# Reordering the first two units of a fused attention and two-layer kernel

## The chip, the core and the metric

One Trainium2 (trn2) chip, one core. The metric is the device time of one execution in microseconds (us); 521.43 us is the median of three runs of the kernel before (520.35 to 522.20). Engines: PE (TensorE), DVE (VectorE), ACT (ScalarE), POOL (GpSimd), SP (SyncE, which here only issues DMAs). Each takes its instructions strictly in the order in which they stand in its queue.

## What is computed

A recurrent gated attention over 2 batches, 8 heads, 768 steps and 40 channels, and then two feed-forward layers over the resulting 1536 rows of 320 channels, with 1536 hidden channels each:

```python
for t in range(S):                       # attention, per batch and head
    m_new  = max(f[t] + m, i[t])
    f_stab = exp(f[t] + m - m_new); i_stab = exp(i[t] - m_new)
    C = f_stab * C + i_stab * outer(v[t], k[t]);  n = f_stab * n + i_stab * k[t]
    y[t] = sigmoid(o[t]) * (C @ q[t]) / max(abs(n @ q[t]), 1)
x  = y as rows;  xn = x / rms(x) * rms_g
x2 = (silu(xn @ w_gate) * (xn @ w_val)) @ w_out          # first layer
out = (sigmoid(x2 @ w2_gate) * (x2 @ w2_val)) @ w2_out   # second layer
```

## The kernel before

**Units.** The attention is cut into 12 units: 6 chunks of 128 steps, times 2 batches; unit u is chunk u // 2 of batch u % 2. A unit loads its operands (`a_load`: qk, nat, qt), turns gate sums into weights (`a_bcast_pe`, then `a_exp`; chunk 0 uses `a_bcast0`/`a_bcast0b`), multiplies queries by keys on PE (`a_scores`, L323), weighs the scores on DVE (`a_weigh`, L330), multiplies by the values (`a_out`, L343), makes its addition to the running state (`a_wv` on POOL L289, `a_state` on PE L368, `a_update` on DVE L379), normalises (`a_norm1`, `a_norm1b`, `a_norm1c`, `a_norm2`, `a_norm3`: L391 to L419), is turned by three PE transposes (`a_flip`, L423 to L425) and split into a high and a low part (`a_xt`: ACT L430, DVE L431 and L432). Two units make one tile `xT` of 256 columns; without both, the first layer can't start on it.

**Gate sums.** Those of chunk 0 are made for u = 0 and 1 at once, those of the other chunks by `g_rest`, cut into three bf16 parts by `g_part` (ACT and DVE), and written by `g_send` (L204) as six small DMAs into `rows3[0]` and `rows3[1]`: in the kernel before the three of batch 0 on SP, the three of batch 1 on POOL. `a_bcast_pe` and `a_scale` read these rows. `g_dec` and `g_cols` make the decay factors and columns for the later chunks.

**Weight words.** Each layer has 12 blocks m of weights, each in two pieces p. A piece is loaded by SP (`w_load`, L95, 544 KB) into one of four buffers `wraw`, unpacked by two ACT passes (`w_pre`: L99 and L106) and a DVE pass (`w_bits`, L110), after which its `wraw` buffer is free, and split into wH on ACT (`w_hi`, L119) and wL on DVE (`w_lo`, L123), after which its `wT` buffer (three of them) is free. So load k + 4 waits for `w_bits` of piece k. Pieces are named (layer, m, p); piece k of the first layer is (0, k // 2, k % 2).

**First layer.** Steps are pairs (group g of 256 rows, block m): 16 `up` matmuls (L460), tanh and products on ACT, DVE and POOL (`act1`), two steps later 6 `down` matmuls (L471 to L473). Groups 0 to 3 each go through all 12 blocks in turn, so in group 0 each step also has to wait for its block's weights.

**What sets the order.** Up to the first matmul of group 0 all engines follow an order written out by hand (L637 to L751). `keep_warm(n)` (L685) puts n matmuls without use into PE's queue; `T["wm"]` has their numbers. After the last instruction of that order on each engine (`marks`) a planner orders everything else at compile time, by due times (`want`) and by its own estimate of when operands are ready; `unit(u)`, `w_step(k)` and the `up`, `down` steps give those due times. PSUM tiles named `at`, `up`, `sc` and `dn` have two buffers each; a new tile takes the one that comes free first.

**Names in the steps.** Units 0 and 1 are chunk 0 of the two batches. In PSUM, `at` holds in turn the outputs of `a_out`, `a_state`, `a_flip` and `g_cols`, and `up` holds both the sums of `a_bcast_pe(2)` and those of the first steps.

Of the kernel before, what the change touches and what calls it, by code (L numbers as in the profile page):

```python
# [16 lines left out]
B, H, S, D = 2, 8, 768, 40  # L17
# [33 lines left out]
    start=9.89, d0=4.6, d1=2.84, d2=5.36, w0=1.9, w1=-11.36, wld=9.1, lead=(33, 35, 35, 35, 42, 60), skew=3.0, stg=1.5,  # L51
    uld=9.62, sl=9.1, fl=-6.46, wm=(6, 5, 4, 8, 4), st=1.2,
    fs=(2, 3, 5, 6, 14, 16),
# [4 lines left out]
def attention_then_two_moe(tc, fi, fir, qk, qt3, nat, w1, w2, rms_g, consts, out):  # L58
# [141 lines left out]
    def g_send():  # L200
        n = H * NR
        for k in range(3):
            for b, q in ((0, nc.sync), (1, nc.gpsimd)):
                q.dma_start(out=rows3[b][k * n:(k + 1) * n].rearrange("p q l -> p (q l)"), in_=parts[b * n:(b + 1) * n, k])  # L204

# [396 lines left out]
    def w_step(k):  # L602
        moe, m, p = piece(k)
        if k < 3:
            return
        t = t_slot(first(moe, None, m)) + T["w1" if moe else "w0"] + p
        if k > 3:
            want(t - T["wld"], lambda: w_load(moe, m, p))
        want(t - 3, lambda: w_pre(moe, m, p))
        want(t - 2, lambda: w_bits(moe, m, p))  # L610
        want(t - 1, lambda: w_hi(moe, m, p))
        want(t, lambda: w_lo(moe, m, p))

    def unit(u):
        t = t_unit(u) + (u % B) * T["skew"]
        st = [
            [a_scale, a_bcast_pe, a_exp],
            [a_scores, a_wv, a_gate],
# [18 lines left out]
    with tc.manual_schedule(engines=set(engines)):  # L637
# [78 lines left out]
        a_weigh(1)  # L716
        a_state(0)
        w_pre(0, 0, 1)
        g_part(1)
        a_norm1b(0)  # L720
        a_norm1c(0)
        g_send()
        a_out(1)
        a_norm2(0)
        w_hi(0, 0, 0)
        a_gate(1)
        w_bits(0, 0, 1)
        a_norm3(0)
        keep_warm(wm[2])
        a_flip(0)  # L730
        a_norm1(1)
        a_norm1b(1)
        a_norm1c(1)
        a_xt(0)
        w_lo(0, 0, 0)
        w_hi(0, 0, 1)
        g_dec()
        a_update(0)
        a_norm2(1)
        w_pre(0, 1, 0)  # L740
        keep_warm(wm[3])
        g_cols()
        a_norm3(1)
        keep_warm(wm[4])
        a_flip(1)
        w_lo(0, 0, 1)
        a_xt(1)
        w_bits(0, 1, 0)
        w_hi(0, 1, 0)
        w_lo(0, 1, 0)  # L750
        marks = [next(i for i in reversed(nc.cur_bb.bb.instructions) if i.engine == e) for e in engines]  # L751

# [113 lines left out]
```

## Time and profile before

| | value |
| --- | --- |
| median of three runs | 521.43 us |
| the profiled execution | 520.35 us |
| its span, first to last instruction | 518.6 us |
| PE busy | 505.1 us, 97% |
| ACT, DVE, POOL busy | 231.3, 261.0, 108.7 us |
| bytes read from HBM | 39.10 MB |
| first `up` matmul | 36.34 us after the start of the span |

The span is what the trace covers; 1.75 us of the profiled execution lie around it. Times in the rows are us from the start of the span. Busy shares are averages over stages that have different limits, so the page's share by engine says little about the first 100 us; the views that cut the span into stretches do. A matmul's shown duration contains a modelled end that overlaps the next one.

### The profile page before, as it was taken

What the parts mean: (1) busy time and instruction counts of PE and PEld (TensorE: products, weight loads), DVE (VectorE), ACT (ScalarE), POOL (GpSimd) and SP (SyncE); (2) the same over time, 40 slices, a digit from 0 to 9 for tenths busy, and PEclk for the clock granted to TensorE, in tenths of its full rate; (3) what the DMA queues carried; (4) which work ended last, traced back from release to release, by engine and by line L of the source; (5) the groups of instructions that cost most, each with busy time, mean ns of one, the idle gap of its engine ahead of it and who ended that gap; (6) DMA issues with size and microseconds to landing.
All of it is one profiled execution on the core that took longest, in us unless ns stands there. A gap on an engine that the chain in (4) does not pass through costs nothing.

```text
span 518.6 us, 9096 instructions
## 1 busy us (share of the span) xinstructions
PE 505.1 (97%) x3592; PEld 467.3 (90%) x3592; DVE 261.0 (50%) x540; ACT 231.3 (45%) x518; POOL 108.7 (21%) x173
## 2 busy tenths in 40 slices
PE   9879998999999999999999999999999999999997
PEld 6758897999999999999999999998888888888997
DVE  5677999643355445547675646523233233222332
ACT  4568998632243233326577556442222222221332
POOL 5432252632233343222221212110000000000000
PEclk9789999999999989999999999999999999999999
DMA  7777878510021020102053341000000010000100
GB/s 235 224 237 239 280 256 274 189 59 1 27 81 55 25 81 15 42 1 87 25 196 126 108 151 44 1 1 25 1 1 2 0 52 0 1 1 0 52 1 25
DMA packets 15366, 41.83 MB, mean 81 GB/s; under 512 B 1898, under 2 KB 6613, under 8 KB 15324
## 3 DMA queue, kind: packets, MB, share of 16 engines
q1 hardware_dynamic: 15036, 40.92, 24.3%
q8 instruction: 28, 0.46, 0.4%
q10 hardware_dynamic: 192, 0.25, 0.1%
q0 software_dynamic: 96, 0.09, 0.1%
q14 instruction: 14, 0.11, 0.1%
HBM read 39.10 MB, written 1.97 MB: 79 GB/s over the span
## 4 chain that ended last, share of the span: by engine, by line
PE 75%; DMA 10%; ACT 8%; DVE 4%; issue 2%; POOL 0%; SPq 0%; ACTq 0%; POOLq 0%
PE up L460 32%; PE sc L460 9%; DMA wraw<-in_w_dram 9%; PE dn L471 5%; PE dn L472 5%; PE dn L473 5%; PE at L343 4%; PE sc L323 3%; ACT wT L99 2%; ACT wH L119 2%; ACT wraw L106 2%; PE dn L685 2%; DVE wT L110 2%; PE at L472 2%; PE at L471 2%
## 5 line engine op out<-in xcount | busy, mean ns | idle before, releaser
L460 PE MATMUL up<-xT,wH 128*128 128x256 f32 x940 | 163.7, 288 | 3.8 <-DVE th L491 1.8
L460 PEld LDWEIGHTS up<-xT,wH 128*128 128x128 f32 x940 | 134.8, 190 | 6.8 <-DVE th L491 3.7
L460 PE MATMUL up<-xT,wL 128*128 128x256 f32 x564 | 101.6, 287 | 0.1
L493 POOL TENSOR_TENSOR hT<-th,hT 128x256 fp32r<-128x256 f32 x72 | 58.5, 813 | 144.7 <-ACT hT L492 105.1
L460 PEld LDWEIGHTS up<-xT,wL 128*128 128x128 f32 x564 | 82.1, 191 | 0.6 <-DVE wL L123 0.3
L471 PE MATMUL dn<-wH,hT 128*128 128x320 f32 x184 | 58.0, 316 | 0.0
L472 PE MATMUL dn<-wL,hT 128*128 128x320 f32 x184 | 57.1, 311 | 0.0
L473 PE MATMUL dn<-wH,hT 128*128 128x320 f32 x184 | 56.3, 314 | 0.7 <-POOL hT L493 0.7
L490 DVE SCALAR_TENSOR_TENSOR th<-th,up 128x256 f32<-128x256 f32 x72 | 30.0, 417 | 53.1 <-ACT th L489 52.6
L544 ACT ACTIVATE th<-up 128x256 f32<-128x256 f32 (+1 forms) x48 | 23.6, 491 | 72.4 <-PE up L460 72.4
L545 DVE SCALAR_TENSOR_TENSOR th<-th,sc 128x512 f32<-128x512 f32 x24 | 16.5, 688 | 64.0 <-PE sc L460 63.9
L546 ACT CAST hT<-th 128x256 fp32r<-128x256 f32 (+1 forms) x48 | 24.6, 513 | 50.8 <-DVE th L545 50.8
L489 ACT ACTIVATE th<-up 128x256 f32<-128x256 f32 x72 | 27.4, 381 | 41.8 <-PE up L460 41.8
L106 ACT ACTIVATE wraw<-wraw 128x544 int32<-128x544 uint16 x48 | 33.9, 709 | 22.6 <-DMA wraw<-in_w_dram 22.5
L492 ACT CAST hT<-th 128x256 fp32r<-128x256 f32 x72 | 29.1, 404 | 32.5 <-DVE th L491 32.5
L547 DVE TENSOR_TENSOR hT<-th,hT 128x256 fp32r<-128x256 f32 (+1 forms) x48 | 28.3, 589 | 25.0 <-ACT hT L546 24.9
L110 DVE SCALAR_TENSOR_TENSOR wT<-wT,wraw 128x544 int32<-128x544 int32 x48 | 36.3, 766 | 5.8 <-ACT wT L99 5.1
L123 DVE TENSOR_TENSOR wL<-wT,wH 128x544 fp32r<-128x544 f32 x46 | 33.2, 755 | 9.8 <-ACT wH L119 9.6
L471 PEld LDWEIGHTS dn<-wH,hT 128*128 128x128 f32 x184 | 34.7, 188 | 1.5 <-ACT hT L492 0.2
L472 PEld LDWEIGHTS dn<-wL,hT 128*128 128x128 f32 x184 | 34.6, 188 | 0.9
L473 PEld LDWEIGHTS dn<-wH,hT 128*128 128x128 f32 x184 | 34.0, 188 | 1.2 <-POOL hT L493 0.9
L99 ACT ACTIVATE wT<-wraw 128x544 f32<-128x544 f32 x48 | 32.9, 703 | 0.4 <-DVE wL L123 0.2
(191 smaller groups left out, 831.1 us busy)
## 6 DMA issues: line engine op xcount, KB each, us to landing
wraw<-in_w_dram SPq DMA_DIRECT2D x48, 544.0 KB
nat<-in_nat_dram SPq DMA_DIRECT2D x12, 324.0 KB
qk<-in_qk_dram SPq DMA_DIRECT2D x24, 160.0 KB
nat<-in_nat_dram SPq DMA_DIRECT2D x12, 180.0 KB
qt<-in_qt_dram SPq DMA_DIRECT2D x10, 180.0 KB
out_dram<-x2n SPq DMA_DIRECT2D x11, 160.0 KB
gB<-in_rms_g_dram SPq DMA_DIRECT2D x1, 160.0 KB
out_dram<-x2n ACTq DMA_DIRECT2D x1, 160.0 KB
```

The costliest lines, as they stand in the source:

```text
L99: nc.scalar.activation(t.bitcast(F32), wraw[moe, m, p][:, :, 1].bitcast(F32), AF.Prelu, scale=2.0 ** -112, alpha=2.0 ** 32)
L106: nc.scalar.activation(raw[:, :, 0], top, AF.Copy, scale=2.0 ** -13, bias=2.0 ** -14 - 0.5)
L110: nc.vector.scalar_tensor_tensor(out=t, in0=t, scalar=3, in1=raw[:, :, 0], op0=ALU.logical_shift_left, op1=ALU.bitwise_or)
L123: nc.vector.tensor_tensor(out=wL[moe, m][:, sl], in0=wT.pop((moe, m, p)).bitcast(F32), in1=wH[moe, m][:, sl].bitcast(F32), op=ALU.subtract)
L460: mm = nc.tensor.matmul(o, lhsT=a, rhs=b, start=(n == 0), stop=(n == 7))
L471: nc.tensor.matmul(o, lhsT=hi, rhs=wo[0], start=first, stop=False)
L472: nc.tensor.matmul(o, lhsT=hi, rhs=wo[1], start=False, stop=False)
L473: pe_last[0] = nc.tensor.matmul(o, lhsT=lo, rhs=wo[0], start=False, stop=last)
L490: nc.vector.scalar_tensor_tensor(out=th, in0=th, scalar=1.0, in1=gt, op0=ALU.add, op1=ALU.mult)
L492: nc.scalar.copy(hT[:, 0, :], th)
L493: nc.gpsimd.tensor_tensor(out=hT[:, 1, :], in0=th, in1=hT[:, 0, :].bitcast(F32), op=ALU.subtract)
L547: nc.vector.tensor_tensor(out=hT[:, 1, :], in0=th, in1=hT[:, 0, :].bitcast(F32), op=ALU.subtract)
```

## The change

In the order written by hand: `a_state(0)` moves from before unit 1's output to after `a_norm1(1)`; `a_norm1b(0)` and `a_norm1c(0)` move behind the output of unit 1 and `w_hi(0, 0, 0)`; the first pass over piece (0, 1, 0) moves forward; the normalisation of unit 1 moves ahead of `a_norm3(0)` and of `w_hi(0, 0, 1)`; `a_bcast_pe(2)` and `a_exp(2)` are taken out of `unit(2)` into the hand order; `g_dec`, `a_update(0)` and `g_cols` move behind `a_xt(1)`; piece (0, 1, 1) is unpacked and split by hand too. All six DMAs of `g_send` are issued by POOL. Of the warm-up matmuls, group 2 has 3 instead of 4 and group 3 has 6 instead of 8.

```diff
-    uld=9.62, sl=9.1, fl=-6.46, wm=(6, 5, 4, 8, 4), st=1.2,
+    uld=9.62, sl=9.1, fl=-6.46, wm=(6, 5, 3, 6, 4), st=1.2,
@@ g_send
-            for b, q in ((0, nc.sync), (1, nc.gpsimd)):
-                q.dma_start(out=rows3[b][k * n:(k + 1) * n].rearrange("p q l -> p (q l)"), in_=parts[b * n:(b + 1) * n, k])
+            for b in range(B):
+                nc.gpsimd.dma_start(out=rows3[b][k * n:(k + 1) * n].rearrange("p q l -> p (q l)"), in_=parts[b * n:(b + 1) * n, k])
@@ w_step
-        if k < 3:
+        if k < 4:
             return
         t = t_slot(first(moe, None, m)) + T["w1" if moe else "w0"] + p
-        if k > 3:
-            want(t - T["wld"], lambda: w_load(moe, m, p))
+        want(t - T["wld"], lambda: w_load(moe, m, p))
@@ unit
-            [a_scale, a_bcast_pe, a_exp],
+            [a_scale, a_bcast_pe, a_exp] if u > B else [a_scale],
@@ the order by hand
         g_part(0)
         a_norm1(0)
         a_weigh(1)
-        a_state(0)
         w_pre(0, 0, 1)
         g_part(1)
+        g_send()
+        keep_warm(wm[2])
+        a_out(1)
+        w_hi(0, 0, 0)
+        a_gate(1)
         a_norm1b(0)
         a_norm1c(0)
-        g_send()
-        a_out(1)
+        w_pre(0, 1, 0)
+        w_bits(0, 0, 1)
         a_norm2(0)
-        w_hi(0, 0, 0)
-        a_gate(1)
-        w_bits(0, 0, 1)
-        a_norm3(0)
-        keep_warm(wm[2])
-        a_flip(0)
         a_norm1(1)
+        a_state(0)
+        keep_warm(wm[3])
         a_norm1b(1)
         a_norm1c(1)
+        a_norm3(0)
+        w_hi(0, 0, 1)
+        a_flip(0)
+        a_norm2(1)
+        w_lo(0, 0, 0)
+        w_pre(0, 1, 1)
         a_xt(0)
-        w_lo(0, 0, 0)
-        w_hi(0, 0, 1)
-        g_dec()
-        a_update(0)
-        a_norm2(1)
-        w_pre(0, 1, 0)
-        keep_warm(wm[3])
-        g_cols()
+        a_bcast_pe(2)
+        keep_warm(wm[4])
         a_norm3(1)
-        keep_warm(wm[4])
         a_flip(1)
         w_lo(0, 0, 1)
         a_xt(1)
+        a_exp(2)
+        g_dec()
+        a_update(0)
+        g_cols()
         w_bits(0, 1, 0)
         w_hi(0, 1, 0)
+        w_bits(0, 1, 1)
         w_lo(0, 1, 0)
+        w_hi(0, 1, 1)
+        w_lo(0, 1, 1)
```

## Rows read from the trace of the kernel before

**Rows 1.** The page, part 1: busy time of PE, share, instructions.

```profile
PE 505.1 (97%) x3592; PEld 467.3 (90%) x3592; DVE 261.0 (50%) x540; ACT 231.3 (45%) x518; POOL 108.7 (21%) x173
```

**Rows 2.** Stretches: window, length, busy us (count) by engine, granted clock, DMA share, GB/s.

```profile
14.00:36.30 22.30, 17.99 (x123) 13.38 (x121) 16.23 (x37) 12.69 (x33) 7.00 (x11) 0.85 0.70 221
...
20.00:26.60 6.60, 6.60 (x26) 4.29 (x26) 3.82 (x11) 3.63 (x10) 0.98 (x1) 0.50 0.89 274
...
36.30:95.80 59.50, 56.85 (x441) 52.17 (x442) 52.27 (x97) 52.32 (x109) 23.07 (x30) 0.97 0.80 261
95.80:250.00 154.20, 154.17 (x1261) 149.14 (x1260) 76.67 (x187) 57.75 (x150) 50.10 (x79) 0.99 0.15 48
```

**Rows 3.** Chain of waits, 14 to 37 us: start, length, engine, tile, line.

```profile
18.15 1.39 issue
...
30.09 0.61 PE at L368 x6
...
31.58 1.09 PE sc L323 x16
32.67 0.32 PE at L297 x3
...
34.64 0.48 PE at L339 x2
35.12 0.21 PE at L368 x2
35.34 0.43 PE at L339 x4
```

**Rows 4.** Timeline to the first up matmul: start, length, engine, line, operation, [idle before].

```profile
13.84 1.88 PE L343 MATMUL at<-nat,E 128*128 128x41 f32 x16
...
16.84 1.29 DVE L330 TENSOR_TENSOR E<-E,sc 128x512 f32<-128x512 f32 x2 [0.16 <-PE sc L323]
...
18.94 0.49 DVE L403 TENSOR_TENSOR y<-at,rd 128x320 f32<-128x320 f32 x1
...
28.46 1.02 DVE L417 SCALAR_TENSOR_TENSOR y<-y,r,gB 128x320 f32<-128x320 f32 x1
...
29.53 0.33 PE L423 MATMUL at<-ident,y 128*128 128x128 f32 x1 [0.71 <-DVE y L417]
...
30.13 0.48 ACT L430 CAST xT<-at 128x384 fp32r<-128x384 f32 x1 [2.81 <-PE at L425]
...
30.64 0.42 DVE L431 TENSOR_TENSOR xT<-at,xT 128x256 fp32r<-128x256 f32 x1 [0.30 <-ACT xT L430]
...
36.34 0.74 PE L460 MATMUL up<-xT,wH 128*128 128x256 f32 x4 [0.59 <-ACT E L307]
```

**Rows 5.** The same timeline, queues of SP (SPq) and POOL.

```profile
16.11 3.22 SPq L204 DMA_DIRECT2D rows<-x2n  x3
...
18.05 0.52 POOL L204 DMA_DIRECT2D rows<-x2n  x1 [0.90 <-ACT x2n L194]
...
18.88 0.51 POOL L204 DMA_DIRECT2D rows<-x2n  x1 [0.31 <-DVE rd L396]
...
28.40 0.73 POOL L289 TENSOR_TENSOR wv<-nat,early 128x328 f32<-128x328 f32 x1
...
30.84 0.35 SPq L249 DMA_DIRECT2D nat<-in_nat_dram  x1
...
32.22 0.33 SPq L95 DMA_DIRECT2D wraw<-in_w_dram  x1
...
35.24 0.35 SPq L95 DMA_DIRECT2D wraw<-in_w_dram  x1
```

**Rows 6.** The same timeline, second weight block on DVE, load 7 on ACT.

```profile
39.28 1.36 DVE L123 TENSOR_TENSOR wL<-wT,wH 128x544 fp32r<-128x544 f32 x2
...
41.37 0.70 ACT L106 ACTIVATE wraw<-wraw 128x544 int32<-128x544 uint16 x1 [1.57 <-DMA wraw<-in_w_dram]
```

**Rows 7.** DMA issues before 110 us: queue, count, KB each, us to landing.

```profile
rows<-x2n POOLq DMA_DIRECT2D x3, 30.0 KB, 1.8
```

## The prediction

> **What bounds the kernel now.** I read the page first: PE is busy 97% of the span [rows 1], which alone would leave almost nothing to gain. So I cut the span into stretches. From 95.8 to 250 us PE is busy 154.17 of 154.20 us [rows 2]: there PE's own work is the bound, and whatever PE has finished earlier comes off the end. From 36.3 to 95.8 us PE is busy 56.85 of 59.5 us at a granted clock of 0.97, while ACT and DVE show 52.3 us each and the DMA engines 80% [rows 2]: weights are unpacked for the first time there, four resources are nearly full together, and none of them has much to give. From 14 to 36.3 us PE is busy 17.99 of 22.3 us (and part of that is warm-up), ACT only 12.69, DVE 16.23 [rows 2]. This is the stretch that the change rewrites. The chain of waits and the timeline then say what PE did in it, and the queue of SP what was waiting behind what.
>
> The Trainium skill, page "Trainium Kernel Development and Optimization", note on reading a trace, says that matmul busy time is a poor measure because matmuls are pipelined; by it 56.85 of 59.5 us may hide further gaps. The trace agrees in so far as a shown duration contains a modelled tail. The sum below does not use it.
>
> **Part 1: `a_state(0)` behind unit 1's output.** Unit 0's output and its state both sit in the two `at` buffers, so unit 1's `a_out` finds none. Its weighing is done at 16.84 + 1.29 = 18.13 us, but the chain shows 1.39 us of "issue" from 18.15, and the buffer's last reader, L403, ends at 18.94 + 0.49 = 19.43 [rows 3, 4]. With the state behind, the output can start at 18.15 and takes the 1.88 us that unit 0's took at full clock [rows 4]: done at 20.0. After that gap the clock of PE is 0.50 from 20 to 26.6 us [rows 2]; whether it stays up now is open, since PE will again be empty for some 2 us before the first turn. The three warm-up matmuls taken away stand where PE waits for DVE and ACT, so I cost them at nothing; what they cover is the clock, and if it is lost, part 2 pays (last paragraph).
>
> **Part 2: normalisation, turn and `xT`, replayed with the old durations.** ACT now runs the first unpacking of (0, 1, 0), two passes of about 0.70 us [rows 6], before `a_norm1(1)`, so unit 1's absolute values come at 21.9 us, not right behind its output at 20.0, and its normalised rows at about 23.5 on DVE. `a_norm3(0)` stands behind these: first turn at about 24.3 us. ACT then takes `w_hi` (about as long as one unpacking pass), waits for the fourth `wT` buffer until `w_lo(0, 0, 0)` is done (25.2), unpacks piece 3 until 26.5, copies unit 0's `xT` until 27.0, and DVE subtracts until 27.7. `a_norm3(1)` follows; in the row its product took 1.02 us while POOL ran L289 beside it [rows 4, 5], and without this neighbour I take 0.55 (bounds 0.55 and 1.02) and 0.2 for the copy: second turn at 28.5 us against 29.53 [rows 4]. So this part gains about 1 us (bounds 0.3 and 1.5).
>
> **Part 3: `a_bcast_pe(2)` and `a_exp(2)` in front, the largest term.** Before, PE did not go from the second turn to `up`. It ran the state of unit 1, scores, scale, and the parts of unit 2, waited for DVE in between, and then needed an `up` buffer that ACT's exponentials still held: `up` starts at 36.34 us and waits for "ACT E L307" at the end [rows 3, 4], though the split of xT was at 30.64 + 0.42 us, with one more subtraction of some 0.3 behind it. Now the broadcast is ahead of the second turn and the exponentials come right after `a_xt(1)` on ACT. From the turn at 28.5: 0.6 for the transposes, 0.48 on ACT, 0.42 and some 0.3 on DVE [rows 4], and by estimate 0.2 for `g_dec` and 0.4 for `g_cols` and hand-overs gives a first `up` at about 31.0 us: 5.3 us earlier. `g_cols` in front of `up` costs some 0.6 of this, as its matmul waits for `g_dec`, which stands behind the split on DVE.
>
> This isn't 5.3 us off the end. What PE did between the turn and 36.34 is still owed: 0.61 (state of unit 1), 1.09 (scores), 0.32 (scale), 0.48 + 0.21 + 0.43 (output and state of unit 2) [rows 3], 3.1 us. Net, PE is ahead by **2.2 us** when it reaches the same point.
>
> **Part 4: the fourth piece.** wL of (0, 1, 1) was finished at 39.28 + 1.36 = 40.6 us at the latest [rows 6]; now DVE and ACT do it right after `g_cols`: bits at 32.3 to 33.0, high part to 33.7, low part to 34.5 us. Block 1 is then 6 us earlier, which the earlier `up` needs. ACT was idle 22.3 - 12.69 = 9.6 us from 14 to 36.3 us [rows 2]; my replay of the new order leaves 7.0 us (1.3 + 1.5 + 0.5 + 2.3 + 1.4 between the steps above), so ACT enters the crowded stretch **2.6 us** ahead. DVE gains 1 to 2 us in the same way. Loads: load 6 waits for the bits of (0, 1, 0), which come at 32.3 as before (its row is 32.22); load 7 goes from 35.24 to 33.0 us, and ACT waited for that one until 41.37 [rows 5, 6]. So weights, ACT and PE are all ahead by about 2 to 2.6 us, DVE a little less.
>
> **Part 5: `g_send` all on POOL.** Before, SP stood in these issues from 16.11 for 3.22 us [rows 5], and load 4 behind it; now load 4 can go at 15.0. Nobody waits for load 4 (its unpacking starts after 33 us), so I cost the gain at nothing. POOL takes three more issues at 0.51 us [rows 5], until 20.1 us, before its power for unit 0 is asked for at 20.9. The last row lands 1.8 us [rows 7] later, at 22; the broadcast that reads it stands behind the turn at 24.3, so 2 us of cover remain.
>
> The Trainium skill, page "DMA: Bandwidth & Descriptors", section on the anatomy of a gpsimd DMA, gives a fit of 2.0 us plus bytes over 436e3 for one such DMA, 2.1 us here (an estimate from that page); were six taken one after the other from 16.4, the last would land at 28.8 and hold the broadcast by over 3 us. The rows speak against that: the second and third of POOL's issues start 0.83 us apart, 0.52 and 0.51 us long [rows 5], and the three land in 1.8 us at the median [rows 7], so they overlap.
>
> **The sum.** PE ahead by 2.2, ACT by 2.6, DVE by 1 to 2, and from 95.8 us on the lead is kept. I take 2.4 us, as PE and ACT are the two fullest: the profiled execution would go from 520.35 to 517.95. It lies 1.08 us under the median of the runs shown, so for the median 521.43 - 2.4 = **519.0 us**. A measurement of this kernel can tell about 0.3%, 1.56 us, from no change.
>
> **Rivals.**
> *The reserve goes too.* PE shows 59.5 - 56.85 = 2.65 us idle and loses 3% of 59.5 us, 1.8 us, to the clock in the crowded stretch [rows 2]. If blocks 1 to 3 being early removes this, 4.4 us come on top of 2.4 at most: 514.6, I take 515.5. Against it: ACT and DVE are themselves almost full there. Chance 0.10.
> *The lead is given back.* The planner makes a new order for everything behind the hand order, with the same due times, and DVE or the DMA engines, at 80% [rows 2], let later blocks come when they did: PE only waits in another place. Then 521.4. For it: all four are within 12% of each other. Chance 0.24.
> *Weights queue behind `nat` on SP (slower).* Unit 3's `nat` load waits for the state of unit 1, and in the row it stands ahead of load 6 on SP: 30.84, then 32.22 [rows 5]. POOL's L289 for unit 1 now has to follow the two selects of `a_exp(2)`, about 31.7 us, so the state comes at about 33.2, `nat` takes SP until 34.1, and load 6, if it stays behind, goes out 1.9 us late. Weights then set the pace, the early `up` gains nothing, and the end moves to 523.3. It decides if the planner keeps that order and `nat` is free later than 32.3 us. Against it: load 6 has the earlier due time, and will now be ready first. Chance 0.18.
> *The change does not start `up` earlier*, because the planner or a buffer keeps other work ahead of it, belongs to the second rival; its share there is small.
>
> **Chances and range.** The forecast (517.2 to 520.2) has 0.48, the reserve 0.10, given back 0.24, slower 0.18. Faster by over 0.3% (under 519.87): most of the first and all of the second, 0.56. Within 0.3%: 0.26. Slower: 0.18. The range goes from 515.2, which takes in most of the second case, to 522.9, all of "given back" and the edge of the slower one; about a fifth stays outside.
>
> **What would show it.** Right: first `up` near 31 us, no "issue" gap before unit 1's output, second turn near 28.5, wL of (0, 1, 1) before 35, load 6 ahead of unit 3's `nat`, and the end of group 0 (95.8 before) at 93 to 94 us. Wrong: `up` at 31 but the dense stretch still beginning near 96 (given back), or load 6 after 33.5 us (the queue on SP), or a broadcast that waits for the rows. The replay takes the old durations and the clock as it was; if PE stays at 0.50 longer than from 20 to 26.6 us, turns and broadcast come later, and part 2 loses up to 1 us.

## The result, and the profile after

The changed kernel takes **526.34 us** (median of 4 runs, 523.77 to 529.24) against 520.89 us of before beside it (518.49 to 522.20): ratio 1.010, 95% interval 1.005 to 1.015. It is slower by 1%; forecast were 519.0 us, and 515.2 to 522.9 as the range. Ratios, here and below, are the record's estimates over the fast runs and not quotients of the two medians, which take in every run. Its profiled execution took 527.93 us, span 526.2 us, so 7.6 us more span than before.

What the change was to do at the start, it did. Four lines of the timeline after (start, length, engine, line, operation, idle time before it and what ended it):

```profile
18.43 3.47 PE L343 MATMUL at<-nat,E 128*128 128x41 f32 x16
...
25.64 0.38 PE L277 MATMUL up<-pick,rows 120*128 120x512 bf16 x1 [0.21 <-DMA rows<-x2n]
...
28.32 0.30 PE L423 MATMUL at<-ident,y 128*128 128x128 f32 x1 [0.78 <-DVE y L417]
...
29.91 0.74 PE L460 MATMUL up<-xT,wH 128*128 128x256 f32 x4 [1.07 <-ACT E L307]
```

Unit 1's output starts without the 1.39 us of "issue" of [rows 3], the second turn stands at 28.32 us (29.53 in [rows 4]), and the first `up` at 29.91 us, 6.4 us ahead of [rows 4]. Step 1 of group 0 still starts 3.3 us ahead, at 37.16 us (before: 40.45), but step 2 only at 48.28 (before: 45.13). The same view:

```profile
37.16 1.20 PE L460 MATMUL up<-xT,wH 128*128 128x256 f32 x4
...
48.28 1.20 PE L460 MATMUL up<-xT,wH 128*128 128x256 f32 x4
```

Where the time is lost is best read from when each group's result is written into `x2n`, from the timelines of ACT (us from the span's start; the changed kernel is called "after"):

```
                       group 0  group 1  group 2  group 3  group 4    end of span
before                   101.7    148.5    204.1    246.6    340.5       518.6
after                    110.0    154.0    209.4    252.4    347.9       526.2
```

8.3 us are lost in group 0, 2.8 come back in group 1, 1.6 go in group 4. Part of the 8.3 us is only a shift: when group 0 is written, PE has done 702 matmuls after and 659 before, warm-ups left out, and 38 of the 43 more are the attention's. (The 95.8 us that the prediction calls the end of group 0 is the first `up` of group 1, at 95.86 before; after, it stands at 103.03.) Now the stretches of [rows 2] in the kernel after, with 30 to 60 us in slices of 10 us (window, length, busy us of PE, PEld, DVE, ACT, POOL, granted clock, DMA share, GB/s):

```profile
14.00:36.30 22.30, 20.24 (x123) 16.59 (x123) 15.03 (x37) 13.29 (x34) 9.00 (x15) 0.73 0.59 175
30.00:40.00 10.00, 10.00 (x57) 9.35 (x58) 7.88 (x17) 6.42 (x13) 3.36 (x5) 0.56 0.43 136
40.00:50.00 10.00, 10.00 (x69) 8.59 (x67) 6.41 (x12) 7.58 (x15) 3.94 (x5) 0.84 0.78 248
50.00:60.00 10.00, 10.00 (x60) 8.91 (x60) 7.48 (x13) 6.05 (x13) 1.83 (x3) 0.75 0.61 205
36.30:95.80 59.50, 58.03 (x416) 53.00 (x415) 49.88 (x91) 49.00 (x101) 21.44 (x28) 0.87 0.77 253
95.80:250.00 154.20, 154.02 (x1252) 148.54 (x1252) 77.77 (x186) 56.96 (x149) 48.88 (x75) 0.99 0.17 51
```

and the same three slices of before:

```profile
30.00:40.00 10.00, 7.75 (x64) 6.99 (x64) 7.50 (x14) 8.08 (x15) 2.73 (x4) 0.85 0.78 228
40.00:50.00 10.00, 10.00 (x77) 8.84 (x77) 6.82 (x13) 8.04 (x16) 3.21 (x4) 0.98 0.73 245
50.00:60.00 10.00, 10.00 (x74) 8.65 (x75) 9.75 (x20) 10.00 (x22) 2.74 (x3) 1.00 0.72 234
```

PE isn't idle more, it is idle less: 58.03 of 59.5 us busy against 56.85 of [rows 2]. But from 30 to 60 us it does 186 matmuls at granted clocks of 0.56, 0.84 and 0.75 where before did 215 at 0.85, 0.98 and 1.00. DVE and ACT, 52.3 us each in [rows 2], show 49.9 and 49.0: they aren't the bound. And the earlier `up` is hardly a lead in work. Up to 36.3 us both kernels have run 197 matmuls (first before, then after):

```profile
0.00:36.30 36.30, 30.92 (x197) 22.21 (x197) 24.71 (x57) 18.88 (x49) 15.41 (x40) 0.91 0.73 231
```

```profile
0.00:36.30 36.30, 32.19 (x197) 25.13 (x199) 23.49 (x57) 19.47 (x50) 17.42 (x44) 0.83 0.66 203
```

Without the warm-ups, 27 before and 24 after, that is 170 and 173: the kernel after is three matmuls ahead. Its clock was at half for 12.0 us of the time, from 17.5 to 24.3 and again from 31.1 us on; that of before for 6.8 us, from 20.0 to 26.8. At 60 us it is 21 matmuls behind, at 95.8 us 26.

**An account of the span.** I cut each profiled execution into windows of 2 us and split each into PE's idle time, the clock's loss (busy time times one minus granted clock) and the rest, PE's work at full clock:

```
                    span   work   idle  clock  | 30-110 us: idle, clock | 110-360 us: idle, clock
before             518.6  498.3   13.5    6.7  |   4.9    1.6           |   2.1    1.7
after              526.2  496.4   13.0   16.8  |   1.6   10.1           |   3.6    3.3
a7_early_bits      515.6  496.9   15.5    3.1  |   3.5    0.0           |   2.9    1.7
a10_bits_split     522.4  497.0   16.8    8.5  |   2.9    5.1           |   4.4    3.4
b3_early_bits      522.1  499.0   16.3    6.8  |   5.6    0.0           |   4.2    3.4
d2_after_plan      516.7  497.6   12.4    6.7  |   1.6    5.1           |   1.6    0.0
d1_plan_only       517.4  497.4   14.9    5.1  |   6.2    0.0           |   2.2    0.0
b1_wm              520.0  496.0   14.6    9.4  |   4.6    4.8           |   2.1    1.7
c4_cols_split      520.3  495.2   15.4    9.7  |   2.4    3.3           |   4.0    5.0
b2_send_pool       524.4  496.7   16.2   11.5  |   5.7    5.0           |   1.6    5.1
a8_wm              525.4  498.9   14.9   11.6  |   2.9    6.8           |   4.1    3.1
a2_cols_early      527.2  498.0   22.7    6.5  |   9.5    3.4           |   4.2    1.7
c8_split_warm      527.7  498.4   14.0   15.3  |   4.5    1.7           |   4.2    6.7
a6_exp_plan        528.4  496.1   18.7   13.6  |   4.1   11.4           |   3.6    1.7
```

(The other kernels are the experiments below.) Work is nearly the same in all, 495 to 499 us; the rest of the span is idle time plus clock. Between 30 and 110 us the change takes 3.3 us of idle time away, and the clock takes 8.5 us more. Behind 110 us it loses 1.5 us more in idle time and 1.6 more to the clock. The largest single piece of that stands in one place, where group 4's first `down` needs `sc` buffers that DVE's x2T split still reads. The turns are done at 253.5, but on ACT an unpacking pass stands ahead of the x2T copies, and it waits 0.93 us for its load. Timeline after, ACT and PE, then the windows around it:

```profile
254.10 0.68 ACT L106 ACTIVATE wraw<-wraw 128x544 int32<-128x544 uint16 x1 [0.93 <-DMA wraw<-in_w_dram]
254.68 0.39 ACT L492 CAST hT<-th 128x256 fp32r<-128x256 f32 x1
254.98 0.85 ACT L430 CAST x2T<-sc 128x384 fp32r<-128x384 f32 x2
...
256.36 0.56 PE L471 MATMUL sc<-wH,hT 128*128 128x320 f32 x1 [2.18 <-DVE x2T L432]
```

```profile
254.00:256.00 2.00, 0.18 (x2) 0.00 (x0) 0.50 (x2) 1.90 (x5) 0.85 (x2) 1.00 0.00 0
256.00:260.00 4.00, 3.64 (x16) 3.63 (x17) 1.78 (x5) 0.52 (x2) 0.84 (x2) 0.57 0.00 0
```

Before, this matmul waited for nothing (PE was idle for 0.1 us in all between 160 and 260 us). ACT's copies came there right behind the turns. The source is the same; the planner's order is another. Yet this wait doesn't mark the slow kernels: `a7_early_bits` (2.1 us) and `c4_cols_split` (2.3 us) have it too and take 520.43 us each.

Over all runs the mean granted clock of the span says the same: 0.984 for before (about 80 runs), 0.974 for the changed kernel (4 runs). By the account 0.01 of clock is about 5.2 us of a 520 us span, which is the whole difference of 5.4 us. From run to run within one kernel 0.01 goes with only 3.0 us (pooled over all kernels), and one run of the changed kernel at 0.983 still took 524.74; by that measure the clock is 3 us of 5. So by estimate the clock carries between 3 and 5 of the 5 us. It doesn't carry the loss of every kernel: `b3_early_bits` (below) takes 525.91 us and its profile shows no more clock loss than before, 6.8 us, but 2.8 us more idle time.

### The profile page after: what moved, and what is told of

Its sections match the earlier page's. It is cut to its first block, busy times and chain, and to the rows that moved or that the text cites. A ratio compares the mean times of both kernels' runs of the same rounds, so it can differ in the third digit from the quotient of the medians.

```text
span 526.2 us, 9099 instructions
## 1 busy us (share of the span) xinstructions
PE 513.2 (98%) x3589; PEld 476.4 (91%) x3589; DVE 261.8 (50%) x540; ACT 231.6 (44%) x518; POOL 109.6 (21%) x176
## 4 chain that ended last, share of the span: by engine, by line
PE 71%; DMA 12%; ACT 8%; DVE 5%; issue 2%; DVEq 0%; ACTq 0%; SPq 0%
PE up L460 31%; DMA wraw<-in_w_dram 11%; PE sc L460 8%; PE dn L471 4%; PE dn L473 4%; PE dn L472 4%; PE at L343 4%; PE sc L323 3%; ACT wT L99 2%; ACT wH L119 2%; ACT wraw L106 2%; DVE wT L110 2%; PE at L472 2%; PE at L473 2%; PE at L471 2%
## 5 line engine op out<-in xcount | busy, mean ns | idle before, releaser
L460 PE MATMUL up<-xT,wH 128*128 128x256 f32 x940 | 166.4, 291 | 2.5 <-DVE th L491 1.3
L460 PEld LDWEIGHTS up<-xT,wH 128*128 128x128 f32 x940 | 137.7, 195 | 5.1 <-DVE th L491 2.9
L460 PE MATMUL up<-xT,wL 128*128 128x256 f32 x564 | 103.0, 290 | 0.3 <-DVE wL L123 0.3
L493 POOL TENSOR_TENSOR hT<-th,hT 128x256 fp32r<-128x256 f32 x72 | 56.7, 787 | 150.7 <-ACT hT L492 102.9
L460 PEld LDWEIGHTS up<-xT,wL 128*128 128x128 f32 x564 | 83.6, 195 | 1.2 <-DVE wL L123 0.7
L106 ACT ACTIVATE wraw<-wraw 128x544 int32<-128x544 uint16 x48 | 33.9, 708 | 26.7 <-DMA wraw<-in_w_dram 26.7
L110 DVE SCALAR_TENSOR_TENSOR wT<-wT,wraw 128x544 int32<-128x544 int32 x48 | 37.2, 784 | 7.4 <-ACT wT L99 6.8
```

The lines of the kernel that those rows point to most:

```text
L106: nc.scalar.activation(raw[:, :, 0], top, AF.Copy, scale=2.0 ** -13, bias=2.0 ** -14 - 0.5)
L110: nc.vector.scalar_tensor_tensor(out=t, in0=t, scalar=3, in1=raw[:, :, 0], op0=ALU.logical_shift_left, op1=ALU.bitwise_or)
L460: mm = nc.tensor.matmul(o, lhsT=a, rhs=b, start=(n == 0), stop=(n == 7))
L493: nc.gpsimd.tensor_tensor(out=hT[:, 1, :], in0=th, in1=hT[:, 0, :].bitcast(F32), op=ALU.subtract)
```

## The experiments

Medians stand beside those of before in the same session (520.3 to 521.7); the ratio's interval is in brackets. Theory A in the texts is the release of the weights' loads 6 and 7, theory E VectorE's wait at `g_cols`, theory B the lower clock, theory C the six row transfers on POOL, theory D that the planner's new order costs by itself. Of a moved line the edits show the new place only; `...` stands for lines left out.

**The wait at `g_cols`.** The first thing that the trace after shows out of place is this (timeline, PE, DVE, SP's queue):

```profile
30.71 0.23 PE L215 MATMUL at<-ident,x2n 80*128 80x80 f32 x1
...
32.70 0.44 PE L216 MATMUL at<-early 80*120 80x24 f32 x2
...
33.18 0.24 DVE L217 COPY colR<-at 128x80 f32<-128x80 f32 x1 [2.05 <-PE at L216]
...
33.43 1.35 DVE L110 SCALAR_TENSOR_TENSOR wT<-wT,wraw 128x544 int32<-128x544 int32 x2
...
35.99 1.21 DVE L123 TENSOR_TENSOR wL<-wT,wH 128x544 fp32r<-128x544 f32 x1
```

```profile
34.21 0.33 SPq L95 DMA_DIRECT2D wraw<-in_w_dram  x1
35.89 0.33 SPq L249 DMA_DIRECT2D nat<-in_nat_dram  x1
36.32 0.37 SPq L95 DMA_DIRECT2D wraw<-in_w_dram  x1
```

The `up` steps are not held behind the hand order on PE, so the planner has put the 16 matmuls of step 0 between the two matmuls of `g_cols`. DVE's copies wait 2.05 us for the second, and the bits of (0, 1, 0) and (0, 1, 1) behind them; load 6 goes out at 34.21 us (32.22 in [rows 5]), load 7 behind `nat`. Seven kernels move the bits or the wait.

`a1_bits_first`: the bits ahead of `g_dec`.

```
         a_exp(2)
+        w_bits(0, 1, 0)
+        w_bits(0, 1, 1)
         g_dec()
```

> The changed kernel, with w_bits of pieces (0,1,0) and (0,1,1) moved ahead of g_dec, so that DVE unpacks them before it waits for the matmul of g_cols (L216), which the planner put behind the first 16 up matmuls. Theory A (loads 6 and 7 go out late, at 34.2 and 36.3 us instead of 32.2 and 35.2, because DVE stands behind g_cols; all of group 0 is late by that): load 6 goes out at about 31 us, load 7 within 1 us of it, and at least half of the loss of 5.5 us comes back: 521 to 523.5 us. Theory B (the loss is PE at the lower clock from 30 to 60 us): loads go out earlier, but time stays at 525 to 528 us. Theory C (six software DMAs, rows landing at 25.6 us): no change either, 525 to 528.

525.62 us (522.91 to 530.81, 10 runs), 1.008 [1.003, 1.012]. Loads 6 and 7 go out at 32.8 and 33.9, 1.4 and 2.4 us earlier, and nothing is gained that can be told.

`a2_cols_early`: `g_dec` and `a_update(0)` behind `a_xt(0)`, `g_cols` behind `a_bcast_pe(2)`.

```
         a_xt(0)
+        g_dec()
+        a_update(0)
         a_bcast_pe(2)
+        g_cols()
```

> The changed kernel, with g_dec, a_update(0) and g_cols ahead of the second turn as they were before (behind a_xt(0), g_cols behind a_bcast_pe(2)). It takes the wait of DVE away and lets unit 1's and 3's state columns come early too. Theory A: load 6 at about 31 to 32 us, wv of unit 3 ready by 32, and 520 to 523 us. Theory B or C: 525 to 528. The first up should start at 30 to 31 us in any case.

533.46 us (528.93 to 537.62, 4 runs), 1.016 [1.007, 1.024], the slowest of all, though DVE waits only 0.57 us for L216 and the loads go out at 31.8 and 32.9. Its idle time is 22.7 us; one wait alone, in the plan behind:

```profile
42.00 0.58 PE L339 MATMUL at<-St,qt 120*128 120x123 f32 x2 [4.81 <-DVE qt L300]
```

`a7_early_bits`: bits of (0, 1, 0) behind `w_lo(0, 0, 0)`, bits of (0, 1, 1) ahead of `g_dec`.

```
         w_lo(0, 0, 0)
+        w_bits(0, 1, 0)
         w_pre(0, 1, 1)
...
         a_exp(2)
+        w_bits(0, 1, 1)
         g_dec()
```

> The changed kernel with w_bits(0,1,0) behind w_lo(0,0,0), in a stretch where DVE waits from 25.2 to 26.9 us, and w_bits(0,1,1) behind a_xt(1). Load 6 can go at about 26 us, into a stretch where the DMA engines are nearly empty (27 to 34 us). Theory A, carried further: load 6 at 26, load 7 at 31, the whole weight stream 2 to 6 us earlier than in the kernel before, and 516 to 520 us. If the weights are not what sets the pace in group 0 but ACT, DVE or PE are, it stays within 1 us of the kernel with the bits moved less far. Theory B or C: 525 to 528.

520.43 us (517.31 to 528.29, 10 runs), 0.997 [0.994, 1.000]: the loss is gone. Load 6 goes out at 24.96, group 0 ends at 99.0, and the clock stays at 1.00 from 30 to 110 us.

`b3_early_bits`: the kernel before, with the first pass of (0, 1, 0) moved forward and its bits behind `a_norm1c(1)`.

```
         a_gate(1)
+        w_pre(0, 1, 0)
...
         a_norm1c(1)
+        w_bits(0, 1, 0)
```

> The kernel before with one thing of the changed one, carried further: w_pre(0,1,0) forward behind a_gate(1), and w_bits(0,1,0) behind a_norm1c(1), so that load 6 can go at about 25 us instead of 32.2 with everything else in its old place. Theory A (in group 0 the moment at which the wraw buffers come free sets how early the weights arrive): the DMA engines have no gap from 28.8 to 32.2 us, steps of group 0 from m = 3 on come 2 to 4 us earlier, and 517 to 519.5 us. If ACT and DVE are the bound in group 0 whatever the loads do: 520.5 to 522.5 us.

525.91 us (522.75 to 529.72, 7 runs), 1.010 [1.006, 1.014]: slower than before, with load 6 at 25.93. Theory A falls here: earlier loads alone don't make the kernel faster, though the order behind them is new here too.

`c3_cols_first`: the first `up` must stand behind `g_cols` on PE, as my replay had it.

```
+    class LastPE:
+        ins = marks[4]
+    pe_last[0] = LastPE
```

> The changed kernel with one wait added: TensorE's first up-projection must stand behind the two `g_cols` matmuls (L215, L216), the place that my prediction silently gave it. In the trace of the changed kernel the 16 matmuls of step 0 stand between L215 (30.71) and L216 (32.70), VectorE's copy L217 waits 2.05 us for L216, and both `w_bits` of step 1, the release of loads 6 and 7 and ScalarE's `w_hi` queue behind it. Theory E (this wait starts the loss): the copies come at 31.2 and not 33.18, load 6 at about 32.3 and not 34.21, step 1 of group 0 starts at about 35 and step 2 by 45, group 0 ends at about 97 and the run takes 520 to 523. Theory D (any change of the fixed order makes the planner order everything behind it anew, and the new orders lose about 1% in whatever place): loads earlier, but group 0 or the stretch behind it slow all the same, 525 to 528.

526.36 us (523.97 to 532.19, 4 runs), 1.010 [1.004, 1.016]. The wait is gone and the loads follow (timeline, DVE and SP's queue):

```profile
31.12 0.24 DVE L217 COPY colR<-at 128x80 f32<-128x80 f32 x1
...
32.56 3.57 SPq L95 DMA_DIRECT2D wraw<-in_w_dram  x3
```

Group 0 ends at 102.2, as before, in the profiled execution (524.24); there the 2.3 us wait at group 4's first `down` and 3.3 us of clock (before: 1.7) stand behind 160 us instead.

`c4_cols_split`: the two copies of `g_cols` at the end of DVE's hand order.

```
         w_lo(0, 1, 1)
+        g_cols2(at_g)
```

(`g_cols2` holds the two copies, which `g_cols` no longer makes.)

> The changed kernel with the two copies of `g_cols` (L217, L218) at the end of VectorE's fixed order, behind `w_lo(0,1,1)`; its two matmuls stay where they are on TensorE. Nothing in the fixed order of VectorE then waits for the L216 that stands behind 16 up-projections. Theory E: both `w_bits` of step 1 run at 31.2 to 32.6, loads 6 and 7 are released at about 32 and 33, ScalarE's 2.60 and 0.85 us of idle time at 30 to 34 shrink to about 1, step 2 by 45, run 520 to 523. What it costs is the attention of units 2 and 3, whose decay and state wait for the copies (about 2 us later). Theory D: 525 to 528 with the lead lost elsewhere.

520.43 us (517.38 to 523.08, 10 runs), 0.999 [0.996, 1.002]. The same wait is gone and the loss with it. Had I stopped here, the wait would have passed for the cause.

`c6_bits_and_split`: both repairs, each of which gave 520.43 (the diffs of `a7_early_bits` and `c4_cols_split` together).

> The changed kernel with both repairs: `w_bits(0,1,0)` behind `w_lo(0,0,0)` and `w_bits(0,1,1)` ahead of `g_dec`, and the two copies of `g_cols` at the end of VectorE's fixed order. Each alone gave 520.43. Theory E (both take the same wait, VectorE's 2.05 us for L216, off the weights' path): no more than one of them, 519.5 to 521. Theory A (early release of loads 6 and 7 is worth time by itself): 517 to 519. Theory D: 523 to 526, as a plan not tuned for it.

528.06 us (525.26 to 529.88, 4 runs), 1.011 [1.005, 1.018]. Four kernels have no wait for L216 at all, this one, `c3_cols_first`, `c4_cols_split` and `c8_split_warm` (below); they take 528.1, 526.4, 520.4 and 529.5 us. So the wait's absence doesn't make a kernel fast; `d2_after_plan` (below) has it, 1.22 us long, and is fast. Theory E falls.

**Parts of the change alone, or undone.**

`a5_state_back`: `a_state(0)` again ahead of unit 1's output; every engine's order is otherwise that of the changed kernel.

```
         a_weigh(1)
+        a_state(0)
         w_pre(0, 0, 1)
```

> The changed kernel with a_state(0) back ahead of unit 1's output, so that PE waits 1.4 us for the at buffer again, all other orders the same. If moving the state was worth what the prediction gave it, this is slower than the changed kernel by 0.5 to 1.5 us: 527 to 528 us. If it made unit 2's nat load late (23.4 instead of 20.9 us, with weight load 5 queued behind it on SP) and so cost, it is faster: 523 to 525 us. Theory A by load 6 alone: within 1 us of 526.

524.96 us (523.84 to 526.86, 4 runs), 1.009 [1.006, 1.012]. The move gains nothing that can be told; if anything it costs 1 us. Unit 2's `nat` load does go earlier without it (20.6 us, 23.35 after), as the second of the three cases supposed, but 524.96 and 526.34 with four runs each can't be told apart.

`a4_send_split` and `b2_send_pool`: `g_send` over SP and POOL in the changed kernel, all of it on POOL in the kernel before (the edit of the second; the first has it the other way round).

```
-            for b, q in ((0, nc.sync), (1, nc.gpsimd)):
-                q.dma_start(...)
+            for b in range(B):
+                nc.gpsimd.dma_start(...)
```

> The changed kernel with g_send split over SP and POOL as before; PE's order is the same for the first 656 matmuls. Theory C (six software DMAs, rows landing only at 25.6 us and PE waiting for them): rows land by 21, the broadcast starts at the turn, and 522 to 524 us. Theory A: SP is blocked until 19.4 again, load 4 goes at 19.4 instead of 15.7, load 6 as in the changed kernel: 525.5 to 528 us.

> The kernel before with one part of the change alone: all six row transfers of `g_send` on POOL's queue. The fixed order of the four compute engines is untouched, SP's loads follow without the three stops; the planner's order behind the fixed part changes (about 6% of TensorE's and 13% of VectorE's sequence stands elsewhere). Theory E (the loss is in the changed kernel's own order of VectorE and TensorE at 30 to 34 us): within 0.3% of before, 519 to 522.5. Theory D (any new plan is about 1% worse than this one, whose due times were set for it): 524 to 528, with group 0 reaching step 2 at about 45 as before. If the six transfers on one queue were the cause: rows land late, the broadcast and the first up-projection come more than 1 us later than 36.34.

525.98 us (524.71 to 527.92, 4 runs), 1.011 [1.007, 1.015], and 525.76 us (525.11 to 528.65, 4 runs), 1.010 [1.007, 1.014]. Undone, the part gives nothing back; alone, it costs as much as the whole change. And that isn't through the rows: in `b2_send_pool` the first `up` stands at 35.87, no later than before. The planner's order behind has changed, and the clock is down in a stretch in which PE is never idle (100 to 160 us, before, then `b2_send_pool`):

```profile
100.00:160.00 60.00, 60.00 (x492) 58.10 (x491) 26.24 (x65) 18.84 (x50) 20.45 (x32) 1.00 0.16 47
```

```profile
100.00:160.00 60.00, 60.00 (x433) 56.97 (x432) 23.96 (x56) 17.80 (x47) 17.08 (x28) 0.91 0.12 38
```

`a10_bits_split`: `a7_early_bits` with `g_send` over SP and POOL (the lines with a minus above in place of those with a plus); its PE order is the same for 500 matmuls and differs in 0.2% behind them.

> The best kernel so far (the changed one with `w_bits(0,1,0)` behind `w_lo(0,0,0)` and `w_bits(0,1,1)` ahead of `g_dec`, 520.43) with the row transfers again on SP and POOL in turns. TensorE's order is the same for the first 500 matmuls and differs in 0.2% behind them. Its POOL transfers had made TensorE wait 1.76 us for the last row. Theory: that wait goes, the first up-projection moves from 30.6 to about 29.5, and since the order behind it is the same, 518 to 520 (0.1 to 0.5% below). If a lead at the first up-projection is worth nothing by itself: 520 to 521.

524.50 us (523.64 to 525.32, 4 runs), 1.007 [1.004, 1.009]. The wait for the rows is gone and the first `up` stands at 29.7, as expected, but the clock is at half from 44 to 51 us, and 4 us are lost. The earlier first `up` didn't reach the end here. This pair has the least difference of order among the kernels that differ in time: the median granted clock of the runs is 0.982 against 0.990 of `a7_early_bits`, about 4 us by 5.2 us per 0.01, and the medians are 4.1 us apart. So the clock can take 4 us with PE's order nearly untouched; what in the start brought it on isn't shown.

`a6_exp_plan`: unit 2's broadcast and exponentials back to the planner.

```
-            [a_scale, a_bcast_pe, a_exp] if u > B else [a_scale],
+            [a_scale, a_bcast_pe, a_exp],
...
-        a_bcast_pe(2)
...
-        a_exp(2)
```

> The changed kernel with unit 2's broadcast and exp(2) given back to the planner. TensorE then reaches `g_cols` and VectorE its copies without unit 2's pieces in front, and the first up-projection comes at about 35 to 36 as before. My prediction put the 5.3 us of earlier first up-projection on this part. If that lead is worth nothing or costs (TensorE merely waits for step 2's weights, or the up-projections in front of L216 hold VectorE): 519 to 524, no slower than the changed kernel. If the lead is worth something and the loss is elsewhere: 528 to 531.

530.50 us (526.39 to 531.62, 4 runs), 1.015 [1.008, 1.022]. The first `up` stands at 36.8 again and the kernel is 4 us slower than the changed one. That agrees with a lead that is worth something, though this too is a new order.

**The clock.**

`a3_warm`: five warm-up matmuls behind `a_flip(1)`, where PE waits.

```
         a_flip(1)
+        keep_warm(5)
```

> The changed kernel with five more warm-up matmuls behind the second turn, where PE is empty from 28.8 to 29.9 us. Theory B: the granted clock in the first up steps rises from 0.56 (30 to 40 us) to above 0.8, the first 16 ups take 2 us instead of 2.8, and 522 to 524 us come out. Theory A: up starts 0.5 us later at most, g_cols' matmul ends about 1 us earlier with a faster clock, so load 6 comes up to 1 us earlier: 525 to 527 us.

523.53 us (521.09 to 526.41, 10 runs), 1.004 [1.001, 1.007]. The half clock of 31 to 41 us is gone, and 2.8 us of the 5.4 come back; but the clock is at half from 44 to 51 and from 143 to 154 us instead, and the planner's order is a new one here as well.

`a8_wm`: the warm-ups of before in the changed kernel; every engine's order is otherwise the same, so this is the cleanest of these.

```
-    wm=(6, 5, 3, 6, 4)
+    wm=(6, 5, 4, 8, 4)
```

> The changed kernel with the warm-up numbers of the kernel before (one more behind g_send, two more behind unit 0's state); every engine's order is otherwise the same as in the changed kernel. Theory B (the lower clock of PE at the start and in the first steps is what costs, and the three missing warm-ups bring it on): granted clock in 18 to 26 us back near 1, 523 to 525 us. Theory A (weights late, DMA empty): 525.5 to 528 us, as no load moves.

527.28 us (524.10 to 528.78, 4 runs), 1.012 [1.007, 1.017]. Two windows of it:

```profile
30.00:40.00 10.00, 8.43 (x75) 7.34 (x75) 8.10 (x17) 7.31 (x14) 3.42 (x5) 1.00 0.43 146
40.00:50.00 10.00, 10.00 (x54) 8.57 (x53) 7.44 (x14) 7.54 (x16) 4.19 (x5) 0.67 0.79 239
```

The clock is full where it was 0.56, and also from 16 to 26 us (1.00, 0.66 after), and half from 43 to 54 us instead. Three more matmuls moved the stretch of half clock without taking it away.

`b1_wm`: the reverse, three warm-ups fewer in the kernel before, all orders the same.

```
-    wm=(6, 5, 4, 8, 4)
+    wm=(6, 5, 3, 6, 4)
```

> The kernel before with one part of the change alone: three warm-up matmuls fewer (one in the third group, two in the fourth). Every engine's order is otherwise the same, the planner's too. If the warm-ups set the clock that the loss comes from: mean clock 0.975 to 0.98 and 522.5 to 525. If not: within 0.3% of before, 519.5 to 522.5.

521.30 us (517.86 to 522.67, 10 runs), 0.999 [0.996, 1.003]. Taking the three warm-ups away isn't the cause by itself.

`c8_split_warm`: `c4_cols_split` with five warm-ups behind `a_flip(1)` (the line of `a3_warm`).

> The changed kernel with the two copies of `g_cols` at the end of VectorE's fixed order (520.43 by itself) and five more warm-up matmuls behind `a_flip(1)`, where TensorE stands 1.07 us for ScalarE ahead of the first up-projection. The planner's order behind them is again another (17% of TensorE's sequence). Clock theory (over all runs so far one hundredth of mean granted clock goes with 3.1 us of time): the stretch of half clock at 40 to 46 us of the kernel without them (3.3 us lost) moves or goes, mean clock 0.985 to 0.99, 517.5 to 520. Theory D (the place of the half clock and the stalls are those of the new plan, and come out anyhow): 521 to 526.

529.47 us (527.62 to 531.98, 4 runs), 1.015 [1.009, 1.021]: 9 us slower than without them. The half clock of 39 to 46 us is gone, with a shorter one from 53 to 56 us (1.7 us lost from 30 to 110 us, where it was 3.3), but the new order has 4.2 us of idle time and 6.7 of clock loss behind 110 us.

**The planner's order alone.** One number of the planner is changed (`stg`, the step between the stages of an attention unit), and nothing that is ordered by hand: in the kernel before (`d1_plan_only`) and in the changed one (`d2_after_plan`).

```
-    skew=3.0, stg=1.5,
+    skew=3.0, stg=1.4,
```

> The kernel before with its whole fixed order untouched and one of the planner's numbers changed (`stg`, the step between an attention unit's stages, 1.4 for 1.5 us). All that is fixed by hand runs as before, up to 30 us; the planner's order behind it is another (80% of TensorE's and VectorE's sequence kept, about as far from before as the changed kernel's 79 and 78%). Theory D (a new plan alone costs about 1%): first up-projection within 0.7 us of 36.34, all the same 523 to 530. Theory E, or any cause inside the change's own fixed order: 519.5 to 522.5, as before.

> The changed kernel, fixed order untouched, with the same number of the planner changed (`stg` 1.4). VectorE's `g_cols` copies still wait for the L216 behind the up-projections. Theory D: the time is a draw of this plan, anywhere from 520 to 532, and group 0's end moves by more than 2 us from 110.0 with the first up-projection still at 29 to 31. Theory E (the wait in the fixed order carries the loss): 525 to 528, with step 2 of group 0 not before 46.

`d1_plan_only`: 519.79 us (518.99 to 521.18, 10 runs), 0.998 [0.996, 1.001], as fast as before with a fifth of PE's sequence moved and the first `up` at 37.75 us, 1.4 us later. So a new order isn't always worse. `d2_after_plan`: **519.07 us** (517.50 to 522.34, 10 runs), 0.998 [0.994, 1.002], 7.3 us below the changed kernel, with the same hand order and with the faults of it that I had blamed. The twelve runs of the changed kernel's order (with `a5_state_back` and `a8_wm`) lie between 523.8 and 529.2 us, these ten between 517.5 and 522.3. Timeline of `d2_after_plan` (PE, DVE, SP's queue):

```profile
26.25 0.38 PE L277 MATMUL up<-pick,rows 120*128 120x512 bf16 x1 [1.77 <-DMA rows<-x2n]
...
31.21 0.74 PE L460 MATMUL up<-xT,wH 128*128 128x256 f32 x4 [1.07 <-ACT E L307]
...
33.65 0.24 DVE L217 COPY colR<-at 128x80 f32<-128x80 f32 x1 [1.22 <-PE at L216]
...
34.67 0.33 SPq L95 DMA_DIRECT2D wraw<-in_w_dram  x1
35.20 0.33 SPq L249 DMA_DIRECT2D nat<-in_nat_dram  x1
35.63 0.37 SPq L95 DMA_DIRECT2D wraw<-in_w_dram  x1
```

Load 6 goes out even later than in the changed kernel (34.67, 34.21 there), load 7 at 35.63 (36.32 there), step 2 starts at 47.3, and group 0 ends at 105.8, 4 us behind the kernel before. Then it gains: group 1 ends at 146.5, group 3 at 245.1, group 4 at 337.9 (before: 148.5, 246.6, 340.5). PE is idle for 1.6 us from 30 to 110 us, as in the changed kernel. Windows of `d2_after_plan`, for 30 to 60 and 100 to 160 us:

```profile
30.00:40.00 10.00, 8.43 (x74) 7.24 (x74) 8.00 (x17) 7.21 (x14) 3.42 (x5) 1.00 0.43 152
40.00:50.00 10.00, 10.00 (x57) 8.81 (x56) 7.97 (x14) 7.50 (x16) 3.90 (x5) 0.68 0.70 233
50.00:60.00 10.00, 10.00 (x65) 9.12 (x63) 6.34 (x13) 7.61 (x16) 1.81 (x3) 0.80 0.69 225
100.00:160.00 60.00, 59.98 (x498) 59.17 (x497) 27.07 (x68) 20.62 (x57) 20.95 (x32) 1.00 0.16 50
```

It has one stretch of half clock there (5.1 us lost) where the changed kernel has three (10.1), and from 110 to 360 us neither the wait at `sc` nor any clock loss. `a8_wm`, which runs the changed kernel's plan, has almost the same windows as this one until 50 us, and ends 8.7 us later (spans 525.4 and 516.7): it is 2.8 us behind at the end of group 0 and 6.1 at the end of group 1.

## Why the prediction was wrong, point by point

**First `up` and turns (parts 1 to 3): nearly right.** First turn 24.93 (24.3 forecast), second 28.32 (28.5), first `up` 29.91 (31.0). The 0.6 us for `g_cols` in front of `up` was wrong, as the planner let `up` in between; DVE paid for it with 2.05 us. In part 1 the gap went as said, but the output took 3.47 us at half clock, not 1.88, and was done at 21.9, not 20.0. That cost nothing only because ACT was still unpacking (0, 1, 0) until 21.73: unit 1's absolute values came at 21.93, forecast were 21.9. `a5_state_back` shows no gain from the move.

**Part 4: wrong in every time behind the first `up`, without weight.** wL of (0, 1, 1) was done at 37.2 (34.5 forecast), load 6 went at 34.21 (32.3), load 7 at 36.32 (33.0). I had replayed DVE without the wait at `g_cols`. But `d2_after_plan` has wL at 37.5, load 6 at 34.67 and load 7 at 35.63, and takes 519.07, and `b3_early_bits` has early loads and takes 525.91. These times don't set the end: PE fills them with attention.

**Part 5: the cover was gone, the price small.** The last row did not land at 22 but at 25.6, where PE waited 0.21 us for it (1.77 in `d2_after_plan`). The rule of the Trainium skill that I weighed there ("DMA: Bandwidth & Descriptors", anatomy of a gpsimd DMA; 28.8 by an estimate from it, were they taken one after another) is as far off on the other side: neither one by one nor side by side.

**The leads were there in waits, hardly in work.** I forecast PE 2.2 us ahead; idle time from 30 to 110 us fell by 3.3 us, from 4.9 to 1.6, but at 36.3 us PE was only three matmuls ahead (173 against 170). ACT was to enter the crowded stretch 2.6 us ahead and DVE 1 to 2; from 14 to 36.3 us ACT was busy 0.6 us more than before (13.29 and 12.69) and DVE 1.2 us less (15.03 and 16.23).

**The step that failed is the sum.** It took PE's lead as time off the end: it let the lead stand until the end ("from 95.8 us on the lead is kept") and left the clock as it was; the only price that I put on the clock was up to 1 us, in the turns. In the profiled executions the clock's loss went from 6.7 to 16.8 us, more than the 7.6 us by which the span grew. That doesn't follow from the hand order alone: `d2_after_plan` keeps this, shows 6.7 and takes 519.07. So the sum lacked two terms: the clock, and the planner's new order, which the prediction had only as the rival "given back", at worst with no gain. With a new order the price ran from nothing to 12 us: of 15 further kernels (all but `a5_state_back`, `a8_wm` and `b1_wm`; `a4_send_split` and `a10_bits_split` differ little from the order that they start from), four took 519.1 to 520.4 us and eleven 523.5 to 533.5. The changed kernel, `a5_state_back` and `a8_wm`, which share an order behind the hand order, take 526.3, 525.0 and 527.3. But the order isn't all of it: `a7_early_bits` and `a10_bits_split` have nearly one order and are 4.1 us apart, and the clock differs by about that much.

**The rivals.** *Weights queue behind `nat`* had the right sign (523.3) by the wrong way: load 6 went 2.0 us late, but ahead of `nat` and because of DVE, and it isn't the pace. *Given back* came nearest in its mechanism, a new order behind the hand order, but not in its price: the first `up` of group 1 is at 103.03 us instead of where it was (95.86). Of *the reserve* the idle time went in part (1.5 us of 59.5 left between 36.3 and 95.8 us, 2.65 before), and the clock took more than it held.

**What stays open.** Why one order of the same work keeps the clock up and another doesn't. Stretches of half clock begin after waits of PE (at 256 us right behind 2.18 us of idle time), but also where PE has not been idle for 10 us and more (at 48 us after, at 148 us in `b2_send_pool`), and 0.70 us of idle time at 88 us in `d1_plan_only` bring none. The number of warm-ups moves them and doesn't remove them. The Trainium skill, page "TensorE: Matmul & The Clock Gate", section on a second failure mode of the clock, tells of a kernel whose clock swings because of many short gaps between groups of matmuls. That may be so here: a busy PE of 60.00 of 60 us has modelled ends in it that may hide such gaps, and no run shows them. That the clock, and not something that goes with it, is the cause was read from the account and not tested by itself: no kernel changed the clock and nothing else to a lasting effect; `a10_bits_split` beside `a7_early_bits` comes nearest.

## What to carry to other kernels

Where a planner orders everything behind a piece fixed by hand, an edit of that piece is two changes, and the second can be larger: here the same hand order gave 526.3 and 519.1 us. Separate them before judging either: move one of the planner's numbers with the hand order untouched, in both kernels, and compare how far the times move. And in a kernel in which the matmul engine is busy 97% of the time, put the granted clock into the sum as a term of its own. A repaired wait proves a cause only if a second way of removing the same wait helps too.

## What the runs showed of the hardware that I had not expected

**Small transfers on one queue.** With three 30 KB transfers on SP's queue and three on POOL's, POOL's land in 1.8 us at the median [rows 7], and in `a4_send_split` too (the view has no landing time for SP's); all six on POOL's take 6.4 us after. First the line after, then that of `a4_send_split` (DMA issues before 110 us: count, KB each, us to landing):

```profile
rows<-x2n POOLq DMA_DIRECT2D x6, 30.0 KB, 6.4
```

```profile
rows<-x2n POOLq DMA_DIRECT2D x3, 30.0 KB, 1.8
```

With all six on POOL it is 6.5 us in `b2_send_pool`, 6.9 in `a8_wm` and 7.1 in `d2_after_plan`; with three, 1.8 in `a10_bits_split` as well. With all six on POOL, SP's weight loads also go out earlier, and the DMA engines are fuller (share from 16 to 26 us 0.85 after and 0.97 in `d2_after_plan`; with three on POOL 0.61 before and 0.40 in `a4_send_split`). Which of the two makes them slow wasn't separated.

**The clock.** TensorE's granted clock stands at one of two levels, 0.50 or 1.00 (1.2 and 2.4 GHz). With the same order it falls in other places from kernel to kernel (31 to 41 us after, 43 to 54 in `a8_wm`). From 110 to 160 us, where PE is never idle, its loss comes in portions: none in five of the twenty profiled kernels, 1.7 us in nine, 3.4 in four, 5.1 in two.

**None faster than before.** `d2_after_plan` (519.07, ratio 0.994 to 1.002), `d1_plan_only` (519.79) and the two repairs (520.43 each) can't be told from it.
